# Bucketed attention with a two-layer expert network on one Trainium2 core: weights decoded two tiles per instruction, staged in the ring of V, and new figures in the planner's list

## The chip, the cores and the metric

The kernel runs on one core of a Trainium2 chip. TensorE (PE in the profile, with its weight loads as PEld) multiplies matrices, VectorE (DVE) and ScalarE (ACT) do the elementwise work, GpSimd (POOL) only fills constants, and SyncE (SP) issues nearly all transfers. The metric is the device time of one execution in microseconds (us); lower is better.

## The reference, cut to what matters

```python
B, H, S, D = 4, 8, 768, 64                       # q, k, v; proj is 64 x 6
q_bucket = bits(q @ proj > 0); k_bucket = bits(k @ proj > 0)      # 6 bits each
scores = where(q_bucket == k_bucket, q @ k.T / sqrt(D), -1e9)
attn = softmax(scores) @ v                       # (B, H, S, D)
x = attn.transpose(0, 2, 1, 3).reshape(3072, 512)
h = x @ w_in                                     # 512 x 2048
g = where(h > 0, h, exp(min(h, 0)) - 1)
out = g @ w_out                                  # 2048 x 512
```

The weights arrive as 64-bit floats; the kernel reads them as four 16-bit pieces per number and builds 32-bit floats of them.

## The kernel before

**Tiling.** The 3072 tokens are cut into eight chunks of 384 (half a batch element each). A chunk has four pairs of heads (32 pairs in all, `n`), and a pair has six groups of 128 rows of scores (192 groups, `G`). The network runs on a chunk in sixteen steps `f`: the first layer ("F", line 1192, tile `h`), the nonlinearity on ACT and DVE (lines 1216, 1220, 1223, and the high and low halves through the helpers on lines 358 and 363), and the second layer ("S", line 1244, tile `o`). All large matrix products are done in two 16-bit halves, high and low. While chunk c runs its attention, chunk c-1 runs the network, so the first chunk's attention has no network beside it, and the last chunk's network no attention.

**A pair of heads.** Loads of q and k (lines 620, 630), halves, a transpose by DMA (lines 731, 771; the first pair by TensorE), the bucket bits (line 805, tile `z`, then `zb`) copied by small DMAs under the transposed rows (line 835). Each group: scores (line 946, tile `s` or `so`), the row maximum on DVE (line 969), a bias on DVE (line 986), the exponential on ACT (line 997, tile `pt`), 1/sum (lines 1035, 1036), then high half (358) and low half (363) into `hl`, and a transpose of `hl` by DMA into `PT` (line 1053). When six groups are in, TensorE takes the average `av` (line 1130), and `X` gets its halves. `PT` has two buffers; a pair uses both. The first four pairs turn their probabilities on TensorE instead (`flip`, line 1013) and average in 32 bits (line 1100).

**The weights.** There are 32 tiles of 128 x 512 weights: `w0` to `w15` of w_in, `w16` to `w31` of w_out. For each tile, function `one` adds to the plan: a load of 512 KB on SP (line 464), the top bits on ACT ("top", line 480, into one of three slots of `X`), a join with the low bits on DVE (line 483, into `W`), and four small matmuls on TensorE that bound the norm (line 494, tile `acc`). After the sixteenth and the thirty-second tile a scale follows (lines 507 to 516), and then each tile is split into halves (`split`, tiles `w0s`, `w1s` name the scales). Four staging buffers of one tile hold the raw loads: three in `U` (ring "U"), and one at the end of `W` (ring "raw", every fourth tile). `U` serves later as the buffers `e`, `hp` and `g` of the network; `unstaged` makes the network's first steps wait for just the tiles that lay there.

**V.** The ring "v" has seven buffers of the pool `vpool`: the raw v of a head pair (`vf`, line 853) and its halves (`vhl`).

**What sets the order.** Nothing is scheduled at run time: class `Plan` walks all operations with a cost for each (`took`, `late`, `slow`) and a due time, and writes out one instruction order per engine. An operation allowed on two engines ("AV": ACT or DVE) goes where the plan finds it earlier. Each engine then works off its own order, and so does SP: an instruction that waits holds up all that stand behind it on its engine. `o.end` of a transfer is planned as its start on SP, plus 950 ns and `late`, plus 1000 ns and `slow`; a `bulk` load is held back while the planned transfers are more than `BACKLOG` ahead. While TensorE would stand idle in the first 32 us, the plan fills the gap with dummy matmuls (`spin`).

Of the kernel before, what the change touches and what calls it, by code (L numbers as in the profile page):

```python
# [36 lines left out]
VD = -40  # L37
YIELD = (900.0, 2500.0)
# [17 lines left out]
class Op:  # L56

    __slots__ = ("engs", "eng", "run", "took", "late", "due", "deps", "after", "new", "left", "next", "start", "free", "end", "slow", "bulk", "cols", "name")
# [8 lines left out]
class Plan:  # L67
# [4 lines left out]
    def add(self, engs, run, took, due, deps=(), after=(), new=(), use=(), late=0.0, slow=0.0, bulk=False, cols=128, name=""):  # L72
        o = Op(
            engs=engs, eng=None, run=run, took=dict(zip(engs, took if type(took) is tuple else (took,))), late=late, due=due, deps=[d for d in deps if d], after=[a for a in after if a],
            new=list(new), slow=slow, bulk=bulk, cols=cols, name=name,
# [6 lines left out]
    def seen(self, o, e):  # L82
        return o.free if o.eng == e and e != "S" else o.end
# [20 lines left out]
    def order(self):  # L104
# [22 lines left out]
        while len(done) < len(ops):  # L127
            best = None
            for e, waiting in open_.items():
                at, some = None, []  # L130
                for o in waiting:
# [4 lines left out]
                    if e == "S" and o.bulk:  # L136
                        t = max(t, dma - BACKLOG)
# [27 lines left out]
            if e == "S":  # L165
# [34 lines left out]
def lsh_attention_moe(  # L200
# [34 lines left out]
    vpool = ctx.enter_context(tc.tile_pool(name="vpool", bufs=7))  # L235
# [12 lines left out]
        for name, cap in (  # L248
            ("av", 1), ("s", 1), ("so", 1), ("h", 2), ("pp", 8), ("PT", 2), ("x16", 2 * NP), ("v", 7), ("K", NP), ("O", 3),
# [4 lines left out]
            ("sg", 4), ("top", NP * HALF // SL),  # L254
# [15 lines left out]
    def staged_at(t, at):  # L270
        halves = t.bitcast(I16)[:, 2 * at : 2 * at + 4 * SL + 4]
        return {
            "in": halves[:, 1 : 1 + 4 * SL],
            "low": t.bitcast(I32)[:, at : at + 2 * SL].rearrange("p (n x) -> p n x", x=2)[:, :, 1],
            "top": halves[:, 4:].bitcast(BF16).rearrange("p (n x) -> p n x", x=4)[:, :, 0],
        }
# [4 lines left out]
    tops = X[:, NP:].rearrange("p a b -> p (a b)").rearrange("p (a b) -> p a b", b=SL)  # L281
# [18 lines left out]
    area["raw"] = [staged_at(flat(spare(1, 2 * SL + 2)), 0)]  # L300
    RAW = top[0]
# [139 lines left out]
    in_u = []  # L441

    def weight_ops():
# [4 lines left out]
        def one(i):  # L448
            o = int(i >= NSI)
            place = i + 1 + o  # L450
            raw = i % 4 == 0 and (place + 1) * SL <= RAW
            t = buf("raw" if raw else "U")
            d = W[:, place, :]
            di = d.bitcast(I32)
            if o == 0:
                g, kt = i // KT, i % KT
                src = wi64[kt * P : (kt + 1) * P, 4 * g * SL : 4 * (g + 1) * SL]
            else:
                src = wo64[(i - NSI) * P : (i - NSI + 1) * P, :]
            due = i - 14.0 + 0.4 * o * (i - NSI)  # L460

            def load():
                t.t = area["raw" if raw else "U"][t.slot]
                nc.sync.dma_start(t.t["in"], src)

            l = add("S", load, 460.0, due - 6, after=([first_k["q"]] if i == 2 else []) + staged[-1:], new=[t], late=1600.0, slow=1000.0, bulk=True, name=f"w{i}load")
            staged.append(l)
            if not raw:
                in_u.append(i)
            met = [u for a, z, users in regions if a < (place + 1) * SL and place * SL < z for u in users]  # L470
            if (place + 1) * SL > RAW:
                met += raw_users
            if raw:
                raw_users.append(l)

            h = buf("top")

            def top_():
                h.t = tops[:, h.slot]
# [5 lines left out]
            m = add("A", top_, act(SL) + 110.0, due, [l, zeroed], new=[h], use=[t], name=f"w{i}top")  # L485
            s = decoded[i] = add("V", join, vec(SL), due, [m, *met], use=[t, h], name=f"w{i}or")

            def bound():
# [3 lines left out]
                for x in range(SL // P):  # L492
# [3 lines left out]
                        stop=i in (NSI - 1, NSI + NSO - 1) and x == SL // P - 1,  # L496
                    )

            b = add("P", bound, 230.0, due - 40, [s] + ([maxes["seen"]] if i == NSI else []), after=bounds[o][-1:], late=160.0, name=f"w{i}sum")
            bounds[o].append(b)  # L500
            if raw:
                raw_users.append(s)
# [21 lines left out]
        def zero():  # L524
            nc.gpsimd.memset(X[:, NP:], 0.0)
# [848 lines left out]
```

## Time and profile before

| | |
|---|---|
| time, median of 3 runs | 857.09 us (855.75 to 858.48) |
| the profiled execution's own time | 857.44 us |
| its span | 855.7 us |
| TensorE matmul busy | 815.4 us (95%) |
| VectorE busy | 678.9 us (79%) |
| ScalarE busy | 707.0 us (83%) |
| GpSimd busy | 4.8 us |
| DMA engines, mean busy share of q1 | 72.5% |
| mean granted TensorE clock | 0.996 |

The span is what the profile's times count from; the device time of the same execution is 1.7 us longer. Busy TensorE is an average over stages: the first chunk (to about 110 us), the seven chunks in which attention and network run together (to about 780 us), and the last chunk's network alone.

### The profile page before, as it was taken

What the parts mean: (1) busy time and instruction counts of PE and PEld (TensorE: products, weight loads), DVE (VectorE), ACT (ScalarE), POOL (GpSimd) and SP (SyncE); (2) the same over time, 40 slices, a digit from 0 to 9 for tenths busy, and PEclk for the clock granted to TensorE, in tenths of its full rate; (3) what the DMA queues carried; (4) which work ended last, traced back from release to release, by engine and by line L of the source; (5) the groups of instructions that cost most, each with busy time, mean ns of one, the idle gap of its engine ahead of it and who ended that gap; (6) DMA issues with size and microseconds to landing.
All of it is one profiled execution on the core that took longest, in us unless ns stands there. A gap on an engine that the chain in (4) does not pass through costs nothing. (4 is left out here: it accounts for less than half of the span.)

```text
span 855.7 us, 14941 instructions
## 1 busy us (share of the span) xinstructions
PE 815.4 (95%) x5322; PEld 439.8 (51%) x5322; DVE 678.9 (79%) x1511; ACT 707.0 (83%) x1301; POOL 4.8 (1%) x24
## 2 busy tenths in 40 slices
PE   8897888998999999999999999999999999999997
PEld 3365544554554555555555555545455555555553
DVE  5868999999997877988988788889888777773232
ACT  7789999999987889988988789888888778783543
POOL 2000000000000000000000000000000000000000
PEclk9989999999999999999999999999999999999999
DMA  9769667897889589958888888958877768552101
GB/s 298 191 204 293 200 113 130 164 217 122 169 157 178 112 185 209 201 98 154 173 150 131 144 185 191 212 105 151 154 153 141 130 106 155 99 105 38 38 1 38
DMA packets 364330, 128.21 MB, mean 150 GB/s; under 512 B 339112, under 2 KB 357216, under 8 KB 364256
## 3 DMA queue, kind: packets, MB, share of 16 engines
q1 hardware_dynamic: 363952, 127.13, 72.5%
q8 instruction: 42, 0.69, 0.3%
q14 instruction: 32, 0.26, 0.1%
q10 hardware_dynamic: 304, 0.13, 0.1%
HBM read 35.65 MB, written 6.29 MB: 49 GB/s over the span
## 5 line engine op out<-in xcount | busy, mean ns | idle before, releaser
L1192 PE MATMUL h<-X,W 128*128 128x384 f16 x1536 | 312.0, 326 | 4.1 <-ACT U L1220 4.1
L1244 PE MATMUL o<-W,U 128*128 128x512 f16 x1152 | 307.0, 379 | 0.4 <-DVE U L363 0.4
L997 ACT ACTIVATE pt<-pt,nb,sg 128x768 f32<-128x768 f32 x192 | 195.8, 1021 | 41.2 <-DVE nb L986 41.0
L1192 PEld LDWEIGHTS <-W 128*128 128x128 f16 x1536 | 148.3, 97 | 141.8 <-issue 10.3
L969 DVE TENSOR_SCALAR_CACHE_REDUCE pt<-s 128x768 f32<-128x768 f32 x180 | 171.2, 951 | 16.3 <-PE s L946 15.5
L363 DVE SCALAR_TENSOR_TENSOR hl<-pt,r,hl 128x768 f16<-128x768 f32 x168 | 165.2, 1013 | 8.4 <-ACT hl L358 8.3
L1244 PEld LDWEIGHTS <-U 128*128 128x128 f16 x1152 | 110.3, 97 | 101.8 <-issue 2.8
L946 PE MATMUL s<-K,O 128*128 128x384 f16 x720 | 147.8, 327 | 9.8 <-DVE pt L969 9.2
L358 ACT ACTIVATE hl<-pt,r 128x768 f16<-128x768 f32 x168 | 148.8, 928 | 1.0 <-ACT U L358 0.5
L1223 DVE SCALAR_TENSOR_TENSOR U<-U 128x384 f32<-128x384 f32 x128 | 70.9, 554 | 51.2 <-ACT U L1220 50.8
L946 PEld LDWEIGHTS <-O 128*128 128x128 f16 (+1 forms) x768 | 72.9, 98 | 68.5 <-issue 23.3
L1216 ACT ACTIVATE U<-h,ch 128x384 f32<-128x384 f32 x128 | 73.0, 570 | 40.5 <-PE h L1192 39.4
L358 ACT ACTIVATE U<-U,sgg 128x384 f16<-128x384 f32 x128 | 78.1, 610 | 25.6 <-DVE U L1223 25.6
L363 DVE SCALAR_TENSOR_TENSOR U<-U,sgg 128x384 f16<-128x384 f32 x128 | 78.6, 614 | 22.3 <-ACT U L358 19.9
L1130 PE MATMUL av<-PT,vhl 128*64 128x384 f16 x1008 | 90.2, 327 | 6.3 <-DMA PT<-hl 6.3
L1130 PEld LDWEIGHTS <-vhl 128*64 128x64 f16 x1008 | 57.7, 110 | 37.8 <-issue 11.4
L1220 ACT ACTIVATE U<-h,ch 128x384 f32<-128x384 f32 x128 | 72.9, 570 | 0.0
L1035 DVE TENSOR_SCALAR r<-sm 128x2 f32<-128x2 f32 x84 | 13.9, 166 | 30.5 <-ACT pt L997 30.2
L997 ACT ACTIVATION_READ_ACCUMULATOR pt<-pt,nb,sg 128x1 f32 x192 | 36.9, 192 | 0.0
L1013 PE MATMUL flip<-W,pt 128*128 128x128 f32 x144 | 23.6, 287 | 2.4 <-ACT PT L358 1.6
L358 ACT ACTIVATE X<-av 128x384 f16<-128x384 f32 x28 | 13.5, 481 | 13.6 <-PE av L1130 13.4
L363 DVE SCALAR_TENSOR_TENSOR X<-av,X 128x384 f16<-128x384 f32 x28 | 15.5, 554 | 11.3 <-ACT X L358 11.3
(134 smaller groups left out, 581.3 us busy)
## 6 DMA issues: line engine op xcount, KB each, us to landing
U<-in_moe_w_in_dram SPq DMA_DIRECT2D x12, 512.0 KB
vf<-in_v_dram SPq DMA_DIRECT2D x16, 384.0 KB
U<-in_moe_w_out_dram SPq DMA_DIRECT2D x12, 512.0 KB
qst<-in_q_dram SPq DMA_DIRECT2D x30, 192.0 KB
kst<-in_k_dram SPq DMA_DIRECT2D x14, 384.0 KB
out_dram<-W SPq DMA_DIRECT2D x16, 256.0 KB
PT<-hl SPq DMA_TRANSPOSE x168
W<-in_moe_w_in_dram SPq DMA_DIRECT2D x4, 512.0 KB
```

Of the source, the lines that this page charges most:

```text
L358: nc.scalar.activation(o, x, AF.Copy, scale=s)
L363: nc.vector.scalar_tensor_tensor(o, x, s, hi, ALU.mult, ALU.subtract)
L946: nc.tensor.matmul(s.t[:, y, :HALF], O[x][:rows, j * HC + t, :], K[x][:rows, j * NC + y * HC : j * NC + (y + 1) * HC, :].rearrange("p a b ...
L969: nc.vector.tensor_scalar(pt.t.rearrange("p (n e) -> p n e", n=2), s.t[:, :, :HALF], CLAMP, None, ALU.max, ALU.max, accum_out=m.t[:, y : y ...
L997: nc.scalar.activation(pt_.t, pt_.t, AF.Exp, bias=nb.t[:, y : y + 1], scale=sg_of(n), accum_out=sm.t[:, z : z + 1])
L1013: nc.tensor.transpose(hb.t[:, c * P : (c + 1) * P], pt_.t[:, (y * HC + c) * P : (y * HC + c + 1) * P], eye)
L1130: nc.tensor.matmul(av.t[j * D : (j + 1) * D], vs["hl"][p].t[:, j, c, vx, :], PTs[j].t[:, :, px, c, :], start=y == 0, stop=y == 3 * NC - 1,)
L1192: nc.tensor.matmul(h.t, WH[:, g * KT + t, wx, fc * P : (fc + 1) * P], xbuf[NP * ci + t].t[:, xx, :], start=t == 0 and y == 0, stop=t == KT ...
L1216: nc.scalar.activation(e.t, h.t, AF.Exp, scale=c["ch"])
L1220: nc.scalar.activation(hp.t, h.t, AF.Relu, scale=c["ch"])
L1223: nc.vector.scalar_tensor_tensor(e.t, e.t, -1.0, hp.t, ALU.add, ALU.min)
L1244: nc.tensor.matmul(banks[t][:, :DO], g16.t[:, gx, t * P : (t + 1) * P], WH[:, NSI + 1 + f, wx, :], start=f == 0 and y == 0, stop=f == NF - ...
```

## The change

Function `one` becomes `two`: the weights are handled as 16 pairs of tiles. A load brings 1 MB (two tiles), the top is one ACT instruction over 128x1024, the join one DVE instruction over 128x1024, and the bound eight matmuls. There are two staging buffers of a pair: one in `U`, and one in the last three of the seven buffers of V, which becomes one tile `V` of its own; the ring "raw" is gone. The top bits have two slots, one at the end of `U` and one in `X`. The halves of the first batch's v, and the network's first steps, now wait for all joins. A load may be issued from SP or from ACT, as the plan finds better. Finally the planner's figures for transfers change: transposes and small copies are planned longer, and get a `slow` on top (`SLACK`).

```diff
-            ("kst", 2), ..., ("g", 4), ("ot", 2), ("raw", 1), ("U", 3),
+            ("kst", 2), ..., ("g", 4), ("ot", 2), ("U", 2),
...
-            ("sg", 4), ("top", NP * HALF // SL),
+            ("sg", 4), ("top", 2),
...
-    area["U"] = [staged_at(U, i * 2 * SL) for i in range(3)]
+    V = const.tile([P, 7, S], F32, name="V")
+    area["U"] = [staged_at(U, 0), staged_at(V[:, 4:].rearrange("p a b -> p (a b)"), 0)]
+    tops = [U[:, 4 * SL + 2 :], X[:, NP:].rearrange("p a b -> p (a b)")[:, : 2 * SL]]
...
-        def one(i):
+        def two(i):
...
-                nc.sync.dma_start(t.t["in"], src)
+                (nc.scalar if e == "A" else nc.sync).dma_start(t.t["in"], src.rearrange("(t p) e -> p t e", t=2))
...
-            l = add("S", load, 460.0, due - 6, ..., late=1600.0, slow=1000.0, bulk=True, name=f"w{i}load")
+            l = add("SA", load, (500.0, 620.0), due - 6, ..., late=3200.0, slow=1000.0, bulk=True, name=f"w{i}load")
...
-            m = add("A", top_, act(SL) + 110.0, due, [l, zeroed], new=[h], use=[t], name=f"w{i}top")
-            s = decoded[i] = add("V", join, vec(SL), due, [m, *met], use=[t, h], name=f"w{i}or")
+            m = add("A", top_, act(2 * SL) + 200.0, due, [l, zeroed], new=[h], use=[t], name=f"w{i}top")
+            s = decoded[i] = add("V", join, vec(2 * SL), due, [m, *met], use=[t, h], name=f"w{i}or")
...
-            b = add("P", bound, 230.0, due - 40, ...)
+            b = add("P", bound, 460.0, due - 40, ...)
...
+SLACK = (1500.0, 1000.0, 500.0)
...
-                    tr = [track(add("S", k_tr, 1700.0, due, [lo], ..., late=2100.0, name=f"k{n}tr"))]
+                    tr = [track(add("S", k_tr, 1900.0 if early else 1800.0, due, [lo], ..., late=2100.0, slow=SLACK[1], name=f"k{n}tr"))]
...
-                tr = [track(add("S", q_tr, 1700.0, due + 1, [lo, dup], ..., late=2100.0, name=f"q{n}tr"))]
+                tr = [track(add("S", q_tr, 2700.0 if early else 2300.0, due + 1, [lo, dup], ..., late=2100.0, slow=SLACK[1], name=f"q{n}tr"))]
...
-            cps.append(add("S", copy, 760.0, due, [s], use=[zb, *use], late=100.0, name=name + "cp"))
+            cps.append(add("S", copy, 820.0, due, [s], use=[zb, *use], late=100.0, slow=SLACK[2], name=name + "cp"))
...
-            a = add("AV", hi, either(2 * NC * D, pointer=True), due, [st["scaled"]], ...)
+            a = add("AV", hi, either(2 * NC * D, pointer=True), due, [st["scaled"], *([] if b else decoded.values())], ...)
...
-                        "S", trp, 1650.0, g + 2.0, [l], ...
+                        "S", trp, 1780.0, g + 2.0, [l], ..., slow=SLACK[0]
...
-            x1 = add("A", expo, ..., [o, so, *met_e], new=[e], use=[h], name=f"E{ci}.{f}")
+            x1 = add("A", expo, ..., [o, so, *met], new=[e], use=[h], name=f"E{ci}.{f}")
```

**SP, from the bit copies of the second head pair to those of the fourth.** `K2_321`, `K2_400` and `K2_503` are the transposed k of the second, third and fourth pair, `O_...` the transposed q, `zb_...` the bucket bits; the loads of weights go to `U_88` and, for the ring "raw", to `W_91`. Before:

```order
L835 DMA K2_321<-zb_429 12x384 x4
L835 DMA O_351<-zb_456 12x384 x2
L731 DMA_TRANSPOSE K1_502<-natk_92 128x12x128
L464 DMA U_88<-in_moe_w_in_dram 128x2048 x3
L630 DMA qst_544<-in_q_dram 128x2x192
L835 DMA K2_400<-zb_533 12x384 x4
L835 DMA O_407<-zb_569 12x384 x2
L771 DMA_TRANSPOSE O_630<-natq_93 128x12x128
L835 DMA K2_503<-zb_641 12x384 x4
L464 DMA W_91<-in_moe_w_in_dram 128x2048
```

After, where `K2_314`, `K2_401` and `K2_443` are the same three pairs and a load brings two tiles, to `U_85` or to the end of `V_87`:

```order
L720 DMA_TRANSPOSE K1_442<-natk_90 128x12x128
L824 DMA K2_314<-zb_430 12x384 x4
L824 DMA O_343<-zb_457 12x384 x2
L461 DMA V_87<-in_moe_w_in_dram 128x2x2048
L461 DMA U_85<-in_moe_w_in_dram 128x2x2048
L760 DMA_TRANSPOSE O_577<-natq_91 128x12x128
L824 DMA K2_401<-zb_569 12x384 x4
L824 DMA O_408<-zb_597 12x384 x2
L461 DMA V_87<-in_moe_w_in_dram 128x2x2048
L619 DMA qst_698<-in_q_dram 128x2x192
L619 DMA qst_700<-in_q_dram 128x2x192
L824 DMA K2_443<-zb_696 12x384 x4
```

Ahead of the fourth pair's copies stood the loads of eight tiles (five had been issued ahead of this place); now it is those of twelve (six ahead of this place), and the transpose of the fourth pair's k stands ahead of the second pair's copies.

**ACT, from the end of the first head pair's exponentials into the second pair's.** `pt_..,sw_..` are exponentials, `PT_..<-flip_..` evictions of turned probabilities. Before, where `X_89<-U_88` is the top of the eighth tile, `w7`, and `sw_681` belongs to the second pair:

```order
L480 ACTIVATE X_89<-U_88 128x512
L358 ACTIVATE PT_577<-flip_623 128x384
L358 ACTIVATE PT_577<-flip_637 128x384
L358 ACTIVATE PT_670<-flip_662 128x384
L358 ACTIVATE PT_670<-flip_666 128x384
L997 ACTIVATE pt_628,sw_681<-pt_628,nb_678,sg_287 128x768
L358 ACTIVATE PT_670<-flip_683 128x384
L997 ACTIVATE pt_660,sw_681<-pt_660,nb_678,sg_287 128x768
L358 ACTIVATE PT_670<-flip_699 128x384
L358 ACTIVATE PT_670<-flip_714 128x384
L354 ACTIVATE natq_93,qkx_735<-qst_544 128x384
```

After, where `X_86<-V_87` and `U_85<-U_85` are the tops of `w6` with `w7` and of `w8` with `w9`, `sw_501` belongs to the first pair and `sw_687` to the second:

```order
L986 ACTIVATE pt_580,sw_501<-pt_580,nb_590,sg_162 128x768
L470 ACTIVATE X_86<-V_87 128x1024
L357 ACTIVATE PT_603<-flip_628 128x384
L357 ACTIVATE PT_603<-flip_636 128x384
L470 ACTIVATE U_85<-U_85 128x1024
L357 ACTIVATE PT_603<-flip_649 128x384
L357 ACTIVATE PT_603<-flip_653 128x384
L986 ACTIVATE pt_633,sw_687<-pt_633,nb_675,sg_281 128x768
L986 ACTIVATE pt_659,sw_687<-pt_659,nb_675,sg_281 128x768
L357 ACTIVATE xw_727<-rows_689,vs_477 128x384
L461 DMA U_85<-in_moe_w_in_dram 128x2x2048
L986 ACTIVATE pt_679,sw_687<-pt_679,nb_742,sg_281 128x768
```

Two tops of two tiles stand where single ones stood, ten tiles instead of eight are decoded ahead of the second pair's exponentials, and the one load that is issued from ACT stands among them.

**ACT, around the average of the eighteenth head pair** (`X_89<-av_5450`, after `X_86<-av_5420`, is the first thing done with it). Before, where `pt_5355` and `pt_5384` are the first two groups of the next pair:

```order
L997 ACTIVATE pt_5355,sm_5397<-pt_5355,nb_5390,sg_4725 128x768
L1220 ACTIVATE U_88<-h_5335,ch_5002 128x384
L997 ACTIVATE pt_5384,sm_5397<-pt_5384,nb_5390,sg_4725 128x768
L358 ACTIVATE U_88<-U_88,sgg_5003 128x384
L358 ACTIVATE hl_5431<-pt_5355,r_5424 128x768
L358 ACTIVATE hl_5442<-pt_5384,r_5424 128x768
L1216 ACTIVATE U_88<-h_5393,ch_5002 128x384
L1220 ACTIVATE U_88<-h_5393,ch_5002 128x384
L358 ACTIVATE U_88<-U_88,sgg_5003 128x384
L358 ACTIVATE natq_93<-qst_5037,qks_5310 128x6x64
L358 ACTIVATE X_89<-av_5450 128x384
```

After, where the first two groups of the next pair are `pt_5299` and `pt_5324`, and the second two `pt_5349` and `pt_5383`:

```order
L357 ACTIVATE hl_5373<-pt_5299,r_5360 128x768
L357 ACTIVATE hl_5381<-pt_5324,r_5360 128x768
L357 ACTIVATE U_85<-U_85,sgg_4933 128x384
L986 ACTIVATE pt_5349,sm_5395<-pt_5349,nb_5389,sg_4647 128x768
L986 ACTIVATE pt_5383,sm_5395<-pt_5383,nb_5389,sg_4647 128x768
L1199 ACTIVATE U_85<-h_5363,ch_4932 128x384
L1203 ACTIVATE U_85<-h_5363,ch_4932 128x384
L357 ACTIVATE hl_5462<-pt_5349,r_5458 128x768
L357 ACTIVATE hl_5464<-pt_5383,r_5458 128x768
L357 ACTIVATE U_85<-U_85,sgg_4933 128x384
L357 ACTIVATE natq_91<-qst_5095,qks_5228 128x6x64
L357 ACTIVATE X_86<-av_5420 128x384
```

Two exponentials of the next pair stood ahead of this average, and four do now. On TensorE it stood behind three groups of scores of the next pair and stands behind five; over the 27 pairs from the fifth to the thirty-first that is 3.7 groups on average before and 4.7 after.

## Rows read from the trace of the kernel before

**Rows 1.** Stretches, length: busy us of PE, PEld, DVE, ACT, POOL; clock, DMA, GB/s

```profile
20.00:45.00 25.00, 20.51 (x144) 9.58 (x141) 21.15 (x57) 17.65 (x33) 0.00 (x0) 0.96 0.78 185
45.00:80.00 35.00, 30.76 (x227) 19.68 (x227) 26.04 (x65) 29.58 (x60) 0.00 (x0) 0.93 0.77 242
80.00:110.00 30.00, 25.56 (x215) 17.03 (x215) 28.48 (x69) 29.60 (x63) 0.00 (x0) 1.00 0.66 204
110.00:140.00 30.00, 24.28 (x158) 12.68 (x157) 29.69 (x66) 30.00 (x54) 0.00 (x0) 1.00 0.72 132
140.00:180.00 40.00, 36.85 (x235) 19.99 (x234) 39.51 (x81) 39.30 (x71) 0.00 (x0) 1.00 0.86 170
180.00:240.00 60.00, 56.97 (x389) 29.98 (x387) 56.80 (x128) 58.05 (x108) 0.00 (x0) 1.00 0.89 167
...
260.00:580.00 320.00, 315.75 (x2078) 170.20 (x2073) 268.34 (x599) 277.76 (x512) 0.00 (x0) 1.00 0.84 162
...
760.00:848.00 88.00, 88.00 (x495) 46.61 (x494) 31.99 (x60) 44.23 (x81) 0.00 (x0) 1.00 0.15 32
```

**Rows 2.** Waits of TensorE, 110 to 240 us: us in total, times, longest

```profile
PE s L946 <- DVE pt L969: 6.1, 6, 1.5
PE h L1192 <- ACT U L1220: 4.1, 4, 1.2
```

**Rows 3.** Waits of TensorE from 240 us to the end

```profile
PE av L1130 <- DMA PT<-hl: 5.3, 4, 1.7
```

**Rows 4.** ACT in order of time, two tops back to back: start, us, instruction

```profile
17.57 0.77 ACT L480 ACTIVATE X<-W 128x512 f16<-128x512 bf16 x1
18.20 0.77 ACT L480 ACTIVATE X<-U 128x512 f16<-128x512 bf16 x1
```

**Rows 5.** Groups of instructions: form xcount | busy us, mean ns of one | idle before

```profile
L358 ACT ACTIVATE hl<-pt,r 128x768 f16<-128x768 f32 x168 | 148.8, 928 | 1.0 <-ACT U L358 0.5 <-ACT natq L354 0.4
L358 ACT ACTIVATE natq<-qst,qks 128x384 f16<-128x384 f32 x29 | 17.6, 606 | 3.8 <-DMA O<-natq 3.7
L358 ACT ACTIVATE W<-W,w1s 128x512 f16<-128x512 f32 x16 | 11.4, 715 | 0.0
L480 ACT ACTIVATE X<-U 128x512 f16<-128x512 bf16 x24 | 18.6, 781 | 3.7 <-DMA U<-in_moe_w_in_dram 1.9 <-DMA U<-in_moe_w_out_dram 1.8
L483 DVE SCALAR_TENSOR_TENSOR W<-U,X 128x512 int32<-128x512 int32 x24 | 16.3, 688 | 5.3 <-ACT X L480 5.1
L363 DVE SCALAR_TENSOR_TENSOR natk<-kst,qks,natk 128x768 f16<-128x768 f32 x14 | 14.2, 1011 | 0.0
L363 DVE SCALAR_TENSOR_TENSOR natq<-qst,qks,natq 128x384 f16<-128x384 f32 x30 | 18.4, 612 | 0.2
L360 DVE TENSOR_SCALAR W<-W,w0s 128x512 f16<-128x512 f32 x7 | 3.4, 484 | 0.1
L360 DVE TENSOR_SCALAR natq<-qst,qks 128x384 f16<-128x384 f32 x1 | 0.4, 411 | 0.0
```

**Rows 6.** DVE, three joins in a row; ACT's own issues of the two small first loads

```profile
26.03 1.88 DVE L483 SCALAR_TENSOR_TENSOR W<-U,X 128x512 int32<-128x512 int32 x3
...
0.80 1.20 ACTq L401 DMA_DIRECT2D pf<-in_proj_dram  x2
```

**Rows 7.** SP and ACT in order of time: weight loads issued, and tops

```profile
34.68 1.82 SPq L464 DMA_DIRECT2D U<-in_moe_w_in_dram  x3
...
39.34 0.78 ACT L480 ACTIVATE X<-U 128x512 f16<-128x512 bf16 x1 [1.47 <-DMA U<-in_moe_w_in_dram]
...
40.99 0.77 ACT L480 ACTIVATE X<-U 128x512 f16<-128x512 bf16 x1
...
73.23 1.06 SPq L464 DMA_DIRECT2D U<-in_moe_w_out_dram  x2
...
79.20 0.77 ACT L480 ACTIVATE X<-U 128x512 f16<-128x512 bf16 x1 [1.80 <-DMA U<-in_moe_w_out_dram]
...
100.16 0.79 ACT L480 ACTIVATE X<-U 128x512 f16<-128x512 bf16 x1
```

More of the change, by code (lines that the diff above doesn't have):

```diff
@@ L56 @@
 class Op:
-    __slots__ = ("engs", "eng", "run", "took", "late", "due", "deps", "after", "new", "left", "next", "start", "free", "end", "slow", "bulk", "cols", "name")
+    __slots__ = ("engs", "eng", "run", "took", "late", "due", "deps", "after", "new", "left", "next", "start", "free", "end", "slow", "bulk", "dma", "cols", "name")
     def __init__(self, **kw):
@@ L82, in seen @@
     def seen(self, o, e):
-        return o.free if o.eng == e and e != "S" else o.end
+        return o.free if o.eng == e and not o.dma else o.end
     def ready(self, o, e):
@@ L520, in one @@
                 maxes[o] = add("V", scale, 6 * TINY, due - 40, [q_], use=[av], name=f"wscale{o}")
-        raw_users, staged = [], []
+        staged = []
         def zero():
-            nc.gpsimd.memset(X[:, NP:], 0.0)
+            for x in tops:
+                nc.gpsimd.memset(x, 0.0)
         zeroed = add("G", zero, 1500.0, -70, name="tops")
-        for i in range(NSI + NSO):
-            one(i)
+        for i in range(0, NSI + NSO, 2):
+            two(i)
         last = {}
@@ L543, in split @@
             due = NT + LAG - 8 + 1.5 * FG * g + (1.5 * f + 3 if o else 0.1 * (i % KT))
-            a = add("AV", hi, either(SL, pointer=True), due, [decoded[i], maxes[o], *last.get(o, eye_users if o else [])], name=f"w{i}hi")
+            a = add("AV", hi, either(SL, pointer=True), due, [decoded[i // 2 * 2], maxes[o], *last.get(o, eye_users if o else [])], name=f"w{i}hi")
             b = add("V", lo, vec(SL, 1.0, True), due, [a], name=f"w{i}lo")
@@ L778, in prep_ops @@
             else:
-                tr = [track(add("S", q_tr, 1700.0, due + 1, [lo, dup], new=[O], use=[nat1, nat2], late=2100.0, name=f"q{n}tr"))]
+                tr = [track(add("S", q_tr, 2700.0 if early else 2300.0, due + 1, [lo, dup], new=[O], use=[nat1, nat2], late=2100.0, slow=SLACK[1], name=f"q{n}tr"))]
             i["tr"] = tr
@@ L1061, in pair_ops @@
                     add(
-                        "S", trp, 1650.0, g + 2.0, [l], after=[] if make else PT_.users[:1], new=[PT_] if make else [],
-                        use=[hl] + ([] if make else [PT_]), late=2100.0, name=f"tr{g}",
+                        "S", trp, 1780.0, g + 2.0, [l], after=[] if make else PT_.users[:1], new=[PT_] if make else [],
+                        use=[hl] + ([] if make else [PT_]), late=2100.0, slow=SLACK[0], name=f"tr{g}",
                     )
@@ L1204, in moe_ops @@
             e, hp, g16 = buf("e"), buf("hp"), buf("g")
[L1206 to L1212 removed]
+            met = [] if ci else list(decoded.values())
             def expo(e=e, h=h):
```

72 lines of the change are left out of this document (26 added, 46 removed), and 2 rows, old and new, of the table rings.

## The prediction

> **What bounds the kernel now.** I read the stretches first [rows 1]. They show three kernels in one. In the first 80 us no engine is full: VectorE and ScalarE are busy 26.0 and 29.6 of 35 us from 45 to 80, and the DMA engines 77 to 78% of the time; loads, small copies and turns wait for each other. From 80 to 240 us VectorE and ScalarE are both full (126.0 and 127.4 of the 130 us from 110 on), and TensorE is busy 118.1 of those 130 us: it has the network of the first chunks to do, and waits 11.9 us. From 260 us on TensorE itself is full: 315.8 of 320 us, then 88.0 of 88. So after 260 us only what TensorE waits for is worth anything, and before that what VectorE and ScalarE must get through. The next view is TensorE's waits. From 110 to 240 us it waits 6.1 us for VectorE's row maximum, which frees the bank of the scores, and 4.1 us for ScalarE, which frees `h` [rows 2]. From 240 us to the end the largest item is 5.3 us, in four places, for transposes of `hl` into `PT` [rows 3]. The granted clock is at its upper level but for 45 to 80 us (0.93) [rows 1], where TensorE is not the bound, so the clock is no term here.
>
> **The change, part by part.** The profiled execution took 857.44 us, 0.35 us over the median of the runs; all sums start from it.
>
> *Two tiles per instruction.* On ScalarE the tops start 0.63 us apart when back to back [rows 4], so the 32 cost 20.2 us. A top of twice the length is not in the trace. Between the forms with 384 and 768 columns ScalarE takes 0.84 ns per column [rows 5], which for 512 more is 0.43 us, and a pair would take 1.06 us. From above, nothing is saved: 1.26 us. The single top is some 0.07 us longer than the line through those two forms (781 against 713 ns [rows 5]); if that surplus grows with the columns, the pair takes 1.13. I take 1.10, nearest to these two: 16 x 1.10 = 17.6, a saving of 2.6 us. On VectorE three joins in a row take 1.88 us [rows 6] and one alone 0.69 [rows 5], so each adds 0.60; the slope is 1.04 ns per column [rows 5], a pair 1.13, and 16 pairs save 1.1 us of 19.2. The Trainium skill (ScalarE: Activation LUTs, What ACT_TABLE_LOAD costs) gives an ACTIVATE with immediate operands 186 ns and 0.833 ns per element, with an overlap of about 93 ns; this trace's top is 0.11 us longer than that, so the row decides. By the page a pair would save 0.09 us, 1.5 us in all, and the sum below would be 853.0.
>
> *What moves between the engines.* Comparing the two orders, seven operations net that may run on either engine go from ScalarE to VectorE: three of 768 columns, two of 512, two of 384. ScalarE loses 3 x 0.93 + 2 x 0.72 + 2 x 0.61 = 5.5 us [rows 5], less about 0.1 each for the overlap, 4.8. VectorE's forms of them take 0.48 us for 512 and 0.41 for 384 [rows 5]; by the same step 0.63 for 768; together 3.7, less overlap 3.0. One load is issued from ScalarE, at 0.6 us [rows 6]. ScalarE: -2.6 - 4.8 + 0.6 = -6.8 us. VectorE: -1.1 + 3.0 = +1.9 us. Almost all of this lies before 240 us, where both engines are full and feed each other. If ScalarE alone were the bound it would be -6.8, if VectorE alone +1.9; the two are as full as each other [rows 1] and TensorE waits for both [rows 2], so I take the mean: **-2.4 us**.
>
> *The loads and their two buffers.* The bytes are the same, and so is the staging room, four tiles. But a buffer of two comes free only when both are joined. A single load took 4.7 us from the issue of its group to its top, which had waited for it (34.68 to 39.34), and 6.0 us at worst (73.23 to 79.20) [rows 7]. Another 512 KB at the 242 GB/s of that stretch [rows 1] is 2.2 us, so a pair takes 6.9 to 8.2, and with top and join 9.1 to 10.4 us per turn of a buffer; with two buffers one pair each 4.6 to 5.2 us, if nothing waits in a queue, and 5.1 to 5.7 if 1 us is lost in each turn. Before, 24 tiles (`w6` to `w30`) went from 40.99 to 100.16 us [rows 7], which is 4.9 us for two. The place from which this starts is better: ahead of the fourth pair's bit copies twelve tiles are asked for, not eight, and the second pair's exponentials find ten decoded. Four tiles at 2.5 us are 10 us of lead if transfers keep up. Gain and risk are of one size, -5 to +9 us; I take **0**. What waits here is in order: a top that stands before its data holds all exponentials and evictions behind it on ScalarE, and SP's wait for a free buffer holds the bit copies behind it, for which TensorE's scores wait. The new waits for all joins cost nothing as long as the last join comes before the network begins: in both orders the bound of the last tiles stands ahead of, or within one or two groups of scores of, the network's first matmul. If the last join came late, the network's first exponential would wait for it.
>
> *The seven buffers of V.* Three of them hold weights until the last join; the first batch's halves of v now come after that. Before, two of the four high halves were made ahead of the network's first steps on ScalarE, after, three are; no one waits for them earlier than the fifth pair's average, which stands two groups of scores later than it did. Nothing is added: 0.
>
> *The new figures for transfers.* They make the plan put the averages later: 4.7 groups of scores into the next pair instead of 3.7. A group, with what stands between, is some 3.9 us of TensorE, more than the longest of the four waits for `PT`, so where the average moves, that wait goes. But three of the four waits belong to pairs whose average keeps its place (the tenth, fifteenth and twenty-third); only the eighteenth's moves, by two groups. Those three waits depend on how SP's queue stands then, and its order is new all along. A later average also holds the two buffers of `PT` longer. All gone is -5.3; as much again lost elsewhere is +3. I take half: **-2.5 us**.
>
> Sum: 857.4 - 2.4 + 0 - 2.5 = **852.5 us**.
>
> **The rivals.** *VectorE takes over.* TensorE waits longer for VectorE than for ScalarE from 110 to 240 us [rows 2], and VectorE has 4.0 us idle there [rows 1]. If it alone is the bound, its 1.9 us more are added, ScalarE's relief is worth nothing, and the waits for `PT` are exchanged for others: 857.4 + 1.9 - (0 to 2.5) = 857 to 859 us, no change that shows. For it: the row maximum is the longest waiter. Against it: many of VectorE's own instructions follow one of ScalarE's.
>
> *Two buffers of two are too few*, the case on the slow side. It decides from 4.9 us per pair on. At 5.7 us the twelve pairs from `w6` on end 12 x 0.8 = 9 us later, ScalarE stands idle in front of tops from 45 to 110 us, and the first chunk ends as much later, because exponentials wait behind the tops; TensorE has nothing else to do then. 852.5 + 9 = 861.5 us. For it: ScalarE waited 1.5 and 1.8 us for single loads with four buffers [rows 7]. Against it: the lead of four tiles, and the plan reckons with 6 us for a load of two.
>
> *All of it counts.* ScalarE's 6.8 us come through whole and all four waits for `PT` go: 857.4 - 6.8 - 5.3 = 845.3 us. It would need VectorE, at 97% there, to do more in less time.
>
> **How the numbers follow.** About 0.3%, 2.6 us, is what a measurement of this kernel can tell from no change; faster means below 854.5. My forecast, 849 to 855, has a chance of 0.44; all of it 0.06; VectorE takes over 0.28; too few buffers 0.22. Faster: nearly all of the first two, 0.48. Same: 0.30. Slower: 0.22. For 8 in 10 the range runs from 846, just above the best case, to 863, a little above the case of two buffers: 0.08 lies above it and 0.05 below.
>
> **What would show it.** Right: tops near 1.1 us and joins near 1.13 back to back; ScalarE's busy time down by 5 to 8 us and VectorE's up by 1 to 3; the last join between 100 and 108 us; the first network matmul at or before 110 us; TensorE's waits for `PT` after 240 us at 3 us or less. Wrong: ScalarE's idle time in front of tops, 3.7 us before [rows 5], above 8 us with a last join after 110 us would be the buffers; waits of TensorE for the row maximum well above 6.1 us from 110 to 240 us would be VectorE; waits for `PT` above 5.3 us would mean that the new figures, or SP's new order, are no better. The forecast fails as a whole if the first chunk's end shifts by more than 5 us either way, since I took that as 0.

## The result, and the profile after

| | before | after |
|---|---|---|
| time, median | 856.78 us (855.75 to 858.48) | 846.00 us (844.54 to 848.87) |
| the profiled execution's own time | 857.44 us | 848.87 us |
| its span | 855.7 us | 847.1 us |
| mean granted clock | 0.996 | 0.991 |

The ratio is 0.9876 (0.9846 to 0.9907): the changed kernel is faster by 1.24%, 10.8 us. Forecast were 852.5 us in a range from 846 to 863: the sign was right, the gain was more than twice the forecast, and the time lies on the range's lower edge. The execution that was profiled is the longest of its four; the three others had a granted clock of 0.996 to 0.998 and took 844.5 to 846.1 us.

The stretches of after, columns as in [rows 1]:

```profile
80.00:110.00 30.00, 24.10 (x200) 15.87 (x199) 28.09 (x59) 28.06 (x54) 0.00 (x0) 1.00 0.83 258
110.00:140.00 30.00, 20.98 (x115) 10.33 (x113) 27.35 (x63) 25.62 (x44) 0.00 (x0) 0.87 0.51 106
140.00:180.00 40.00, 38.77 (x249) 20.23 (x247) 39.38 (x84) 39.80 (x75) 0.00 (x0) 0.97 0.80 162
180.00:240.00 60.00, 59.33 (x388) 30.72 (x388) 58.83 (x132) 54.98 (x100) 0.00 (x0) 1.00 0.84 154
...
260.00:580.00 320.00, 319.97 (x2123) 171.88 (x2122) 277.81 (x616) 287.68 (x525) 0.00 (x0) 1.00 0.84 164
```

From 80 to 140 us all three engines are emptier than in [rows 1], and the granted clock is 0.87 from 110 to 140 us; TensorE has 45.1 us of work from 80 to 140 us instead of 49.8. From 140 us on it is fuller, and from 260 to 580 us it does not stand still at all, where it stood 4.3 us before. The waits of TensorE from 110 to 240 us, which answer [rows 2]:

```profile
PE s L935 <- DVE pt L958: 9.9, 7, 2.4
PE h L1181 <- DVE X L1102: 0.4, 1, 0.4
PE o L1227 <- DVE U L362: 0.3, 1, 0.3
PE o L1227 <- ACT U L357: 0.2, 1, 0.2
```

The wait for ScalarE's `U` (4.1 us) is gone, that for the row maximum is longer by 3.8. From 240 us to the end the list of TensorE's waits is empty: the 5.3 us of [rows 3] are gone, and so is 1.0 us for a transpose of q. Tops and joins of after, and one top with what ScalarE did next (minimum/median/maximum ns, first and last start; then start, us):

```profile
L470 ACT ACTIVATE U<-U x8: 1346/1360/1405, 17.8 to 100.8; 128x1024 f16<-128x1024 bf16 x8
L473 DVE SCALAR_TENSOR_TENSOR W<-U x8: 1215/1222/1245, 21.4 to 102.2; 128x1024 int32<-128x1024 int32 x8
...
66.78 1.34 ACT L470 ACTIVATE X<-V 128x1024 f16<-128x1024 bf16 x1
67.99 0.85 ACT L357 ACTIVATE PT<-flip 128x384 f32<-128x384 f32 x2
```

A top of two tiles is 1.36 us long and holds ScalarE for 1.21; two single ones in a row took 2 x 0.63 = 1.26 [rows 4].

Two waits of the first 110 us, before and then after, show what tops and joins of two tiles went with there:

```profile
PE acc L494 <- DVE W L483: 4.9, 7, 2.0
PE flip L1013 <- ACT PT L358: 1.6, 4, 0.7
...
PE flip L1002 <- ACT PT L357: 8.8, 11, 1.9
PE acc L484 <- DVE W L473: 0.6, 2, 0.3
```

TensorE waits less for joins, and 7.2 us more for evictions of `flip`, which stand behind tops on ScalarE. (Of the kernels below, f2_tops_single, the same order with each top in two halves, waits 7.5 us for them, and e8_top_price, a new order of the long tops, 4.4: the place in the order counts for more than the length of one top.)

**Where the gain arises.** For every time of the kernel before, I took TensorE's matmuls up to there (columns of first and second layer, averages, scores and bits, each from its recorded start), and looked when the other kernel had got through as many. The difference, averaged from 220 to 260 us, says where a kernel stands there, and the difference at the end says the rest. After stands 1.8 us *behind* at 240 us and 8.6 us ahead at the end. So in these profiles all of the gain, 10.4 us, comes after 240 us. The weights are long decoded by then; of the change, the planner's figures for transposes and small copies are left to act there, and whatever else is new in the order. The experiments tell these apart.

### The profile page after: what moved, and what is told of

It reads as the page before. It is cut to its first block, busy times and chain, and to the rows that moved or that the text cites. A ratio compares the mean times of both kernels' runs of the same rounds, so it can differ in the third digit from the quotient of the medians.

```text
span 847.1 us, 14863 instructions
## 1 busy us (share of the span) xinstructions
PE 814.2 (96%) x5320; PEld 438.9 (52%) x5323; DVE 681.3 (80%) x1502; ACT 703.1 (83%) x1278; POOL 5.2 (1%) x25
## 4 chain that ended last, share of the span: by engine, by line
PE 77%; DVE 10%; ACT 8%; issue 2%; DMA 2%; SPq 1%; POOL 0%; DVEq 0%; ACTq 0%; POOLq 0%
PE h L1181 26%; PE o L1227 26%; PE s L935 12%; PE av L1119 9%; ACT pt L986 2%; DVE pt L958 2%; PE z L794 2%; ACT PT L357 1%; DVE hl L362 1%; PE spin L1320 1%; DVE W L362 1%; DMA qst<-in_q_dram 1%; ACT X L470 1%; ACT hl L357 1%; ACT U L470 1%
## 5 line engine op out<-in xcount | busy, mean ns | idle before, releaser
L1227 PEld LDWEIGHTS <-U 128*128 128x128 f16 x1152 | 110.1, 98 | 104.4 <-issue 6.1
L935 PE MATMUL s<-K,O 128*128 128x384 f16 x720 | 149.3, 330 | 10.3 <-DVE pt L958 10.1
L1206 DVE SCALAR_TENSOR_TENSOR U<-U 128x384 f32<-128x384 f32 x128 | 70.8, 553 | 49.2 <-ACT U L1203 48.7
L362 DVE SCALAR_TENSOR_TENSOR U<-U,sgg 128x384 f16<-128x384 f32 x128 | 78.7, 615 | 21.0 <-ACT U L357 18.4
L1119 PE MATMUL av<-PT,V 128*64 128x384 f16 x1008 | 87.3, 327 | 0.0
L1119 PEld LDWEIGHTS <-V 128*64 128x64 f16 x1008 | 55.6, 110 | 31.2 <-issue 8.4
L1002 PEld LDWEIGHTS flip<-W,pt 128*128 128x128 f32 x144 | 16.4, 145 | 15.8 <-ACT PT L357 12.5
L975 DVE TENSOR_SCALAR nb<-m,sg 128x2 f32<-128x2 f32 x96 | 21.8, 228 | 3.0
```

The lines of the kernel that those rows point to most:

```text
L362: nc.vector.scalar_tensor_tensor(o, x, s, hi, ALU.mult, ALU.subtract)
L935: nc.tensor.matmul(s.t[:, y, :HALF], O[x][:rows, j * HC + t, :], K[x][:rows, j * NC + y * HC : j * NC + (y + 1) * HC, :].rearrange("p a b ...
L1002: nc.tensor.transpose(hb.t[:, c * P : (c + 1) * P], pt_.t[:, (y * HC + c) * P : (y * HC + c + 1) * P], eye)
L1119: nc.tensor.matmul(av.t[j * D : (j + 1) * D], vs["hl"][p].t[:, j, c, vx, :], PTs[j].t[:, :, px, c, :], start=y == 0, stop=y == 3 * NC - 1,)
L1206: nc.vector.scalar_tensor_tensor(e.t, e.t, -1.0, hp.t, ALU.add, ALU.min)
L1227: nc.tensor.matmul(banks[t][:, :DO], g16.t[:, gx, t * P : (t + 1) * P], WH[:, NSI + 1 + f, wx, :], start=f == 0 and y == 0, stop=f == NF - ...
```

## The experiments

My theory: the new figures earn the gain, by starting each average long enough after the last transpose of its probabilities; the pairs of tiles earn nothing. The rivals: the pairs earn it; or any new order of the program moves the time by some us, and this one was lucky. Twelve kernels, five rounds each; a ratio is to the kernel before in the same session, and is not quite the quotient of the two medians (0.984 for e1_figures_alone, for one). The median of before was 856.7 to 858.6 us from session to session, so kernels of different sessions are better compared by their ratios than by their times.

| kernel | ratio (interval) | at 240 us | at the end | from 240 us on | least lead |
|---|---|---|---|---|---|
| before | 1 | 0 | 0 | 0 | 0.3 |
| after | 0.9876 (0.9846 to 0.9907) | +1.8 | -8.6 | -10.4 | 3.2 |
| e1_figures_alone | 0.9825 (0.9793 to 0.9856) | -3.3 | -13.4 | -10.1 | 3.6 |
| e2_pairs_alone | 0.9941 (0.9915 to 0.9968) | +0.6 | -0.1 | -0.7 | 0.6 |
| e3_loads_on_sp | 0.9877 (0.9847 to 0.9907) | -1.3 | -10.5 | -9.2 | 3.1 |
| e4_pt_figures_alone | 0.9861 (0.9830 to 0.9892) | +0.2 | -9.5 | -9.7 | 2.9 |
| k2_kq_alone | 0.9934 (0.9908 to 0.9959) | -2.8 | -5.0 | -2.2 | 0.8 |
| g1_slack_0 | 0.9885 (0.9859 to 0.9912) | -3.3 | -11.5 | -8.2 | 0.5 |
| g2_slack_3000 | 1.0067 (1.0043 to 1.0091) | +3.7 | +7.7 | +4.0 | 4.7 |
| f2_tops_single | 0.9871 (0.9842 to 0.9900) | -2.6 | -13.0 | -10.4 | 3.1 |
| h1_singles_two_queues | 0.9929 (0.9902 to 0.9957) | +6.3 | -4.3 | -10.6 | 3.0 |
| k1_singles_slack_less | 0.9896 (0.9865 to 0.9928) | +2.4 | -8.0 | -10.4 | 2.3 |
| e6_pairs_slack_less | 0.9879 (0.9847 to 0.9910) | -1.1 | -10.2 | -9.1 | 2.7 |
| e8_top_price | 0.9842 (0.9814 to 0.9869) | -3.2 | -12.6 | -9.4 | 3.3 |

The columns in us are of the profiled execution, against that of the kernel before. They come from one execution each, at clocks from 0.987 to 0.998; from 240 to 760 us the clock is 0.99 or 1.00 in all of them, so the column from 240 us on is little touched by that, and the one at 240 us is. *Lead* is the time from the end of the last transpose's issue on SP to the first matmul of that pair's average, the least of all pairs from the tenth on.

### Figures or pairs

All new figures (those of `k_tr`, `q_tr`, `copy` and `trp`, with `SLACK`) on the kernel before:

```diff
-  "S", trp, 1650.0, g + 2.0, [l], ..., late=2100.0, name=f"tr{g}",
+  "S", trp, 1780.0, g + 2.0, [l], ..., late=2100.0, slow=SLACK[0], name=f"tr{g}",
```

> The kernel before (single tiles, four buffers) with the new planner figures for transfers alone. Theory: the gain that lies after 240 us comes from these figures, so all of TensorE's idle time from 240 to 760 us (7.0 us in the kernel before, 0.1 after) goes here too, and its waits for PT there are at most 1 us: 850 us (848.5 to 851.5). Rival, the weights in pairs earn it (less on ScalarE, a better start): 856 to 858, waits for PT of 4 us or more. Rival, any new order moves the time by some us: PT waits partly gone, other waits in their place, 853 to 856.

843.39 us (842.67 to 844.38), ratio 0.9825: 13.3 us less than before. By the ratios this is ahead of the whole change (0.9876), but the two intervals overlap a little. TensorE waits for nothing after 240 us. The size was outside what I expected (848.5 at the least).

The other half, pairs, staging and second queue with the old figures (the same lines back to 1650 without `slow`, and so for q, k and the copies):

> The kernel after with the old planner figures for transposes and small copies, so the pairs of tiles, their staging and the second queue alone. Theory: TensorE's idle time after 240 us is back (4 us or more, most of it waits for PT), the gain of 140 to 240 us stays: 852 to 855 us. Rival, the pairs earn it: 845 to 848, no waits after 240 us. Rival, any new order: anything from 848 to 860, without waits for PT as the main one.

852.90 us (848.61 to 857.41), ratio 0.9941. TensorE's waits from 240 us on are back:

```profile
PE z L794 <- DMA O<-natq: 3.4, 3, 1.8
PE av L1119 <- DMA PT<-hl: 3.2, 3, 1.4
```

So the pairs by themselves are worth about 4 us in the median, and the figures 13; together they gave 10.8, not 17. The two do not add up. The profiled execution is the longest of twelve and shows 0.7 us of gain after 240 us and none before; where the 4 us of the median arise can't be read from it.

### Which figure

Only the two lines of `trp` above, on the kernel before:

> The kernel before with the new figures only for the transposes of the probabilities (their cost on SP, and 1.5 us more until they count as landed); those of q, k and the small copies stay old. Theory: the averages are put later by this figure, which takes TensorE's waits for PT away (5.3 us from 240 us on): 851 to 853 us. Rival, the gain comes from SP's whole order (q and k turned earlier): waits for PT stay above 3 us, 854 to 857.

846.78 us (844.11 to 848.78), ratio 0.9861, better than I expected by 4 us. Up to 140 us this program stays within 0.4 us of the kernel before on average; all of its gain lies after 240 us. The rival is refuted: no wait for `PT` is left, with old figures for q and k.

The rest of the figures, without those of `trp`:

> The kernel before with the new figures for the transposes of q and k and for the small copies alone; the transposes of the probabilities keep their old figure. Theory: their lead before the average stays near the 2.6 us of the kernel before, so TensorE's waits for PT after 240 us stay at 3 us or more, and only the 1 us wait for a transpose of q goes: 853 to 857 us. Rival, the new order of SP that these figures make gives the lead of the probabilities too: PT waits below 1.5 us, 846 to 850 us.

853.04 us (850.93 to 854.17), ratio 0.9934. The wait for q is gone, that for `PT` is not (3.5 us in five places):

```profile
PE av L1131 <- DMA PT<-hl: 3.5, 5, 1.2
PE s L947 <- DVE pt L970: 1.7, 3, 1.1
```

### How much slack

`SLACK[0]` at 0, with all other new figures:

```diff
-SLACK = (1500.0, 1000.0, 500.0)
+SLACK = (0.0, 1000.0, 500.0)
```

> All new figures on the kernel before, but the slack of the transposes of the probabilities is 0 instead of 1500 ns; single tiles as before. Theory: a transpose lands some 2.4 us after its issue ends, and a TensorE average that starts less than that after the last of its transposes waits. The figure sets this lead: 2.6 us on average in the kernel before (0.3 at least), 4.8 us (3.6 at least) with the slack of 1500. With 0 the lead falls back to some 2.8 us, and TensorE waits for PT again, 3 us or more after 240 us: 849 to 853 us. Rival, the other figures or the new order as such had taken the waits away: no PT waits, 843 to 846.

847.18 us (846.21 to 848.81), ratio 0.9885; one wait of 1.6 us for `PT` was left, not 3 us or more. That was a miss in size. Against k2_kq_alone only the planned cost of a transpose on SP differs (1780 ns for 1650). There five pairs from the tenth on have a lead below 2.2 us; here it is one, the tenth (0.5 us), and the 1.6 us are its wait. The order of the whole program is new, though, so that the 0.13 us alone did this is argued and not shown.

At 3000:

> The same with a slack of 3000 ns. Theory: leads of 6 us and more, no wait for PT, and nothing further to gain since TensorE's idle time from 240 to 760 us was 0.1 us with 1500: 842 to 845 us. Rival, averages that stand so late hold the two PT buffers and the next transposes: 847 us or more, with waits of other kinds after 240 us.

863.41 us (861.51 to 865.15), ratio 1.0067: slower than before. The rival was right. Its waits from 240 us on:

```profile
PE h L1193 <- ACT X L359: 4.0, 3, 2.7
PE s L947 <- DVE pt L970: 3.1, 4, 1.2
PE h L1193 <- DVE X L364: 1.9, 3, 1.4
```

No wait is for `PT` (the least lead is 4.7 us), but averages as late as that hold up the network of the next chunk: its first layer now waits for `X`, which is made from the last average (5.9 of the 9.0 us in this list). Against e1_figures_alone it loses 7 us up to 240 us and 14 after; what these waits leave of the 14 was not followed further.

### What the pairs cost and bring

All loads on SP (`add("S", load, 500.0, ...)` for `add("SA", load, (500.0, 620.0), ...)`):

> The kernel after with all loads of weights issued from SP. Theory: one load of 1 MB at 50 us is all that the second queue takes, so 845 to 848 us, no TensorE idle time after 240 us, first chunk within 2 us of that of the kernel after. Rival, the load on ScalarE's queue shortens the first chunk: 849 us or more, with the last join 3 us or more later.

847.52 us (846.42 to 849.77), ratio 0.9877 to after's 0.9876. The second queue, one load of 1 MB, is worth nothing that shows.

Each top of two tiles as two instructions in the same place:

```diff
-  nc.scalar.activation(h.t...[:, :, 1], t.t["top"], AF.Copy)
+  for y in range(2):
+      z = slice(y * SL, (y + 1) * SL)
+      nc.scalar.activation(h.t...[:, z, 1], t.t["top"][:, z], AF.Copy)
```

> The kernel after with each top of two tiles issued as two ACT instructions of 128x512, one behind the other, in the same place; order, loads and joins are unchanged. Theory: the fused top saves next to nothing, since one of 1024 columns takes 1.36 us (1.22 in a row) against 0.63 for a single one in a row: 32 x 0.63 = 20.2 against 16 x 1.22 = 19.5 us, so 846 to 848 us, no difference that shows. Rival, the fused top is worth the 2.6 us of the prediction: 848.5 us or more.

846.12 us (843.98 to 849.23), ratio 0.9871: no difference to after. The long top saves nothing that can be measured. Since the order is that of after, its profile, taken at a clock of 0.998, also shows after at that clock: 2.6 us ahead at 240 us, where after's own profile at 0.991 was 1.8 behind. Some 4 us in the first 240 us go with the clock that an execution is granted; most of them (3.5) are there by 80 us, where the clock from 45 to 80 us is 0.95 in after and 1.00 here.

The second queue on single tiles, with all new figures; five of 32 loads go to ScalarE's queue:

```diff
-  l = add("S", load, 460.0, due - 6, ...)
+  l = add("SA", load, (460.0, 620.0), due - 6, ...)
```

> The kernel before with all new figures and single tiles, and with the loads of weights allowed on ScalarE's queue too (five of the 32 go there). Theory: the second queue is worth nothing here, 842 to 846 us. Rival, it shortens the first chunk: 841 us or less. Rival, issues of 0.6 us on a full ScalarE cost: 846 us or more.

851.15 us (849.58 to 853.15), ratio 0.9929, 7.8 us more than e1_figures_alone: the direction of the last rival, but its price (0.6 us per issue) is not the reason. By the same measure of matmuls this kernel stands 5.5 us ahead of e1_figures_alone at 80 us and 7.2 behind at 110. In between TensorE stands still twice. SP's order, VectorE's, and two waits of TensorE from 80 to 140 us:

```profile
77.50 2.25 SPq L772 DMA_TRANSPOSE O<-natq  x1
79.84 1.08 SPq L465 DMA_DIRECT2D W<-in_moe_w_out_dram  x1
81.15 2.63 SPq L465 DMA_DIRECT2D U<-in_moe_w_out_dram  x2
...
90.30 0.42 DVE L361 TENSOR_SCALAR natq<-qst,qks 128x384 f16<-128x384 f32 x1 [5.90 <-DMA O<-natq]
...
PE rows L1087 <- DVE PT L361: 6.3, 1, 6.3
...
PE z L806 <- DMA O<-natq: 4.0, 1, 4.0
```

A transpose of q, issued at 77.5 us with a load on ScalarE's queue right behind it at 78.7 and more on SP, let VectorE go on only at 90.3. VectorE stood 5.9 us, and an eviction behind it held TensorE for 6.3. The 4.0 us are of the next transpose of q, issued at 92.2, for which TensorE waited until 104.6. A wait of this kind is also there with all loads on SP, in k1_singles_slack_less (below):

```profile
73.42 3.45 SPq L772 DMA_TRANSPOSE O<-natq  x1
76.98 2.07 SPq L465 DMA_DIRECT2D U<-in_moe_w_out_dram  x1
...
82.32 0.61 ACT L359 ACTIVATE natq<-qst,qks 128x384 f16<-128x384 f32 x1 [2.13 <-DMA O<-natq]
```

ScalarE goes on 8.9 us after the issue there, VectorE 12.8 us after it here. So it is not shown that the second queue is the cause.

### Luck of the order

Two neighbours of the figures, 1300, 900 and 400 ns of slack, with single tiles and with pairs:

> Single tiles with all new figures, the three slacks at 1300, 900 and 400 ns instead of 1500, 1000 and 500, a new order of the whole program. Theory: as with 1500 the leads stay above 3 us, no waits after 240 us: 842 to 846 us, and below the kernel with pairs at the same slacks. Rival, an order's luck in the first chunk is worth 3 us and more: anything from 843 to 850.

848.80 us (847.30 to 852.69), ratio 0.9896, outside what I expected.

> The kernel after with the three slacks at 1300, 900 and 400 ns. Theory: pairs cost 2 to 3 us against single tiles at the same figures, in the first chunk, and nothing waits after 240 us: 845 to 849 us. Rival, what pairs cost or gain is an order's luck: anything from 841 to 851, and it may be less than that of the single tiles.

847.59 us (846.23 to 849.43), ratio 0.9879, as expected. But the single tiles were not faster at the same slacks: with 1500 they beat the pairs by 0.5% by the ratios (some 4 us, from two sessions), with 1300 they lose 0.2% (1.2 us by the medians of one session). Both differences arise before 240 us, and the rival can't be refuted: what pairs cost or bring, beside the figures, is not told apart from what any new order of the first chunk moves.

A last one of this kind, after with the top planned at 1.22 us instead of 1.15 (`act(2 * SL) + 270.0`):

> The kernel after, where the plan reckons with 1.22 us for a top of two tiles, as measured in a row, instead of 1.15. Theory: 0.07 us in sixteen places changes the order of the first chunk but not what it has to do: 844 to 849 us. Rival, the plan's short price made TensorE wait for evictions behind tops (8.8 us in the kernel after): waits of that kind at 4 us or less, 843 us or less.

844.55 us (844.29 to 844.86), ratio 0.9842, the best of those with pairs; 844 to 849 was expected. TensorE waits 4.4 us for evictions of `flip`, not 8.8, and stands 3.2 us ahead at 240 us. By the ratios it is 0.3% faster than after, and the intervals overlap.

## Why the forecast had the sign and missed the size

**The new figures: -2.5 forecast, about -10 measured after 240 us.** This is the term that was mis-sized, and two of its reasons were wrong. First, I argued from places in TensorE's order: three of the four waits belong to pairs whose average keeps its place among the groups of scores, so they might stay. What decides is the lead, and it can grow without a change of place. The 23rd pair, before (SP, then TensorE):

```profile
560.72 1.46 SPq L1053 DMA_TRANSPOSE PT<-hl  x1
562.29 3.25 SPq L835 DMA_DIRECT2D O<-zb  x4
565.64 1.44 SPq L1053 DMA_TRANSPOSE PT<-hl  x1
...
567.40 0.35 PE L1130 MATMUL av<-PT,vhl 128*64 128x384 f16 x1
569.35 2.95 PE L1130 MATMUL av<-PT,vhl 128*64 128x384 f16 x34 [1.61 <-DMA PT<-hl]
```

and after, with the average at the same place, four groups into the next pair:

```profile
549.46 3.12 SPq L824 DMA_DIRECT2D K<-zb  x4
552.69 3.43 SPq L1042 DMA_TRANSPOSE PT<-hl  x2
556.21 2.68 SPq L760 DMA_TRANSPOSE O<-natq  x1
...
560.74 2.47 PE L1119 MATMUL av<-PT,V 128*64 128x384 f16 x28
```

Before, four small copies stood between the last two transposes; the issue of the last ended at 567.08, 0.3 us ahead of the average, which waited. After, the two stand together and end at 556.12, 4.6 us ahead. In the kernel before, lead and wait together (from start to start of the matmuls) are 0.4 + 2.0 us in the tenth pair, 0.6 + 1.7 in the fifteenth and 0.3 + 2.0 in the 23rd, so about 2.4 us from the end of its issue is what a transpose mostly needed here; in the eighteenth it was 3.5. It is no fixed figure: the 13th and the 27th average went on with a lead of 1.2 us without a listed wait, behind issues that had themselves taken 2.9 and 3.0 us, not 1.4 to 1.8; and two of the five waits in k2_kq_alone (0.8 and 0.2 us) came with leads of 3.0 and 3.1 us. All kernels in the table without a lead below 2.2 us gained 9 to 11 us after 240 us, but for the one with 3000; g1_slack_0, with one such lead, gained 8.2; k2_kq_alone and e2_pairs_alone, with five each as in before, 2.2 and 0.7.

Second, the list of waits gives less than the waits cost. TensorE's idle time from 240 to 760 us was 7.0 us before and 0.1 after, not 5.3, since waits for q and for the row maximum went too. And part of a wait is booked as busy. A record of a matmul is 0.33 us long, but the next one starts 0.08 us later on average; the first matmul after a wait lies alone and counts whole. The averages and bits from 240 to 760 us, before and then in e1_figures_alone (count | busy us, mean ns | idle before):

```profile
L1130 PE MATMUL av<-PT,vhl 128*64 128x384 f16 x792 | 70.5, 327 | 5.4 <-DMA PT<-hl 5.3
L805 PE MATMUL z<-O,pjz 128*32 128x384 f16 x124 | 8.1, 329 | 1.1 <-DMA O<-natq 1.0
```

```profile
L1131 PE MATMUL av<-PT,vhl 128*64 128x384 f16 x792 | 68.6, 327 | 0.0
L806 PE MATMUL z<-O,pjz 128*32 128x384 f16 x132 | 7.4, 329 | 0.0
```

The same 792 matmuls are 1.9 us shorter, and 132 of `z` 1.2 us shorter than 132/124 of 8.1. In e1_figures_alone TensorE stood idle for 0.2 us there, 6.8 less than before: 6.8 + 1.9 + 1.2 = 9.9 us, close to the 10.1 that e1_figures_alone gained from 240 us on.

**The loss that I set against it, +3 for later averages that hold `PT`:** it didn't come with 1500 ns. It came with 3000, by another way, through `X` and the next chunk's first layer.

**Tops and joins: -2.6 and -1.1.** The join is 1.22 us long; the 1.13 forecast were for one in a row, and a single one alone was longer than in a row by the same 0.09 [rows 5, 6]. The top was not: 1.36 us where 1.10 was taken, in a row 1.21, close to the upper end of 1.26. For 512 more columns it takes 1360 - 781 = 579 ns more, 1.13 ns per column, and not the 0.84 of the forms that I drew the line through [rows 5]. So the tops save 16 x (1.26 - 1.21) = 0.8 us. The saving of 0.09 us per pair, which the prediction worked out from the Trainium skill (ScalarE: Activation LUTs, What ACT_TABLE_LOAD costs), is nearer to these 0.05 us than my 0.16, though the 186 ns and 0.833 ns per element given there would make the long top 1.04 us, and it is 1.36.

**Moves between the engines:** VectorE's busy time rose by 2.4 us (1 to 3 forecast); ScalarE's fell by 3.9 us (5 to 8 forecast), 2.9 less than the 6.8 of the sum, of which 1.8 are what the tops did not save. A wait that came with the new places of the tops had no term in the forecast: TensorE's for evictions of `flip`, 1.6 us before and 8.8 after. Nor had the one that went, for joins, 4.9 before and 0.6 after.

**Loads and two buffers: 0.** ScalarE's idle time in front of tops is 4.6 us, 3.7 before, and the last join starts at 108.6 us, 106.3 before. That rival did not come; it was named for 8 us and 110 us. Two signs of being right were missed by a little: the last join came after 108 us, and the first network matmul at 111.6 us (110.1 before), not by 110.

**The seven buffers of V: 0.** This step looks wrong. Before, two of the three low halves that VectorE made of the first batch's v up to 150 us stood at 70.8 and 111.1 us. After, all wait for the last join, and four instructions on `V` stand right behind it:

```profile
110.41 0.62 DVE L359 TENSOR_SCALAR V<-V,vs 128x768 f16<-128x768 f32 x1
110.94 1.01 DVE L362 SCALAR_TENSOR_TENSOR V<-V,vs 128x768 f16<-128x768 f32 x1
113.42 1.01 DVE L362 SCALAR_TENSOR_TENSOR V<-V,vs 128x768 f16<-128x768 f32 x1
118.45 1.02 DVE L362 SCALAR_TENSOR_TENSOR V<-V,vs 128x768 f16<-128x768 f32 x1
```

That is 3.7 us of VectorE just where TensorE waits for its row maximum; 8.6 of the 9.9 us of that wait lie from 110 to 140 us. In e1_figures_alone no such instruction stands from 97 to 145 us, and the wait from 110 to 240 us is 6.0 us. In e8_top_price, with two such instructions there, 6.6 us of this wait lie from 110 to 140 us; in e1_figures_alone it is 5.1. This was read from the traces; no kernel with just these halves elsewhere was run.

**The clock: no term.** The forecast read it as at its upper level but for 45 to 80 us, though the first line of [rows 1] shows 0.96 from 20 to 45 us as well, and left it out of the sum. In after it was 0.87 from 110 to 140 us. Two profiles of one order, after and f2_tops_single, stand 4.4 us apart at 240 us with mean clocks of 0.991 and 0.998. That is more than the 2.4 us that the forecast moved there.

**The rivals.** *VectorE takes over* had its sign from 110 to 140 us, but the 4.1 us that TensorE had waited for ScalarE went, and from 140 us on after gains. *Too few buffers* did not come (its 12 x 0.8 us are 9.6, not 9, which changes nothing). *All of it counts*, 845.3 us, came nearest in time, with the wrong sum: all waits for `PT` went, but ScalarE's 6.8 us did not come through, and the waits were worth twice their listed time. The first 240 us were worth +1.8 us in after's profile and -2.6 in that of the same order at a higher clock, for a forecast of -2.4; that the latter two are close is luck, since the waits behind them moved in other ways than forecast. The median of after lies on the range's edge because the term of the figures was four times what the sum had for it.

## What to carry to other kernels

Where one engine is full and a written-out order feeds it, read the lead of each transfer over the work that needs it, not only the waits: a plan that counts a transfer as landed too early puts the consumer in front of it, and 0.13 us of planned cost and 1.5 us of slack on one kind of transfer were worth some 10 us here, while 3 us of slack cost 20 us against 1.5. The waits listed for TensorE were less than what they cost: 6.6 us of a gain of 10. And when a new order of a crowded stretch is judged, run a neighbour or two of it: by the ratios, the two neighbours of after lie 0.0 and 0.3% from it, and that of e1_figures_alone 0.7% (some 6 us). What the new weight path is worth beside the figures is not more than that; the best single ratio, 0.9825, is that of the figures on the old weight path.

## What was not expected of the hardware

- ScalarE's copy of every fourth 16-bit number costs 1.13 ns per further column, where 32-bit forms cost 0.84 [rows 5]; joining two such instructions saves 0.05 us.
- TensorE's granted clock fell in a thin stretch even in a kernel that is bound by it: in after it was busy 45.1 of the 60 us from 80 to 140, and the granted clock was 0.87 from 110 to 140 and 0.97 from 140 to 180; from 130 to 135 us it was 0.50, the lower of its two levels, behind 5 us in which TensorE was busy 1.8. How far it falls is not the same each time: f2_tops_single, the same order and busy 44.4 us there, had 0.94 and 1.00. The kernel before alone took 854.3 to 863.3 us over three sessions, at mean clocks from 1.000 down to 0.986.
- A transpose of q with loads behind it was slow to let go. In h1_singles_two_queues the DMA engines were busy for 90% and more from 82.75 to 85 us, and moved 40, 78 and 50 GB/s in the three slices, where 250 GB/s and more went through just before (40 slices of 0.75 us from 76 us on, busy tenths and GB/s below). What limits them there was not found; k1_singles_slack_less, with all loads on SP, shows 32 and 120 GB/s in two slices of 0.35 us behind such a transpose that were busy for 80% and more.

```profile
DMA  8869999599999294899997799899999996201000
GB/s 246 268 186 251 284 271 265 65 152 40 78 50 226 53 124 158 246 350 437 404 382 300 215 287 147 131 107 115 67 77 92 102 132 92 36 31 41 0 0 0
```
